# The second forward twiddle of two convolutions, read in 32 transfers of 1024-byte rows or in 4 of 8192-byte rows

## The chip, the cores and the metric

One core of one Trainium2 chip runs the whole program. The metric is the device time of one execution in microseconds. The engines work in parallel, each in the order of its own instructions: TensorE multiplies matrices (PE in the profile, its weight loads PEld), VectorE (DVE) and ScalarE (ACT) work element by element, GpSimd (POOL) does some set-up, and SyncE (SP) issues the transfers, which 16 DMA engines carry out.

## The reference

The input x has 2048 rows of 512 values. Four residual steps follow each other, two of each kind, with the same weights in both rounds:

```python
x = x + _A_ref(_layernorm(x), wqkv, wo)
x = x + _B_ref(_layernorm(x), A_re, A_im, B_re, B_im, C_re, C_im, log_dt, Dskip)
x = x + _A_ref(_layernorm(x), wqkv, wo)
x = x + _B_ref(_layernorm(x), A_re, A_im, B_re, B_im, C_re, C_im, log_dt, Dskip)
```

Step A is local attention: 32 heads of 16 channels, each position looks at 8 positions (itself and every second one before it). Step B is a long convolution along the 2048 positions, one filter for each of the 512 channels:

```python
P = jnp.exp(logdA[:, :, None] * l[None, None, :])
K = jnp.einsum("dn,dnl,dn->dl", Cc, P, dB).real
Kf, Uf = rfft(pad(K)), rfft(pad(u))
y = irfft(Uf * Kf)[:, :, :L] + u * Dskip
```

## The kernel before

**The stages.** The program first builds the filter K (function k_gen, 0 to about 107 us) together with the first parts of the first attention, then runs attention 1 (LayerA.core, to about 186 us), convolution 1 (FftB, to about 247 us), attention 2 (to about 351 us) and convolution 2 (to the end). The order of the instructions on each engine is written out by hand, as strings of one letter for each operation (CORE0 and CORE1 for the attentions, ORDER0, ORDERF and ORDER1 for the convolutions).

**The convolution.** The Fourier transform of 4096 points is done as two steps of matrix products. The first step (f1, L807) multiplies the data by a fixed 128 x 128 table and leaves 128 groups e for each of 64 sets of channels (a1s). The second step (f2, L814) multiplies each group e by a matrix of its own, 128 x 128: this is the second forward twiddle, a table w2 of 128 x 128 x 128 bf16 values, 4 MB. A call of f2 handles 16 groups (EC), with one weight load and one product for each group. Eight calls cover the 128 groups for one half of the channels. In convolution 1 both the filter (k_f2, letter k) and the data (u_f2, letter u) go through it, 32 calls; in convolution 2 only the data, 16 calls, since the spectrum of the filter is kept in DRAM. Then VectorE multiplies the spectra (u_mult, L852), and two inverse steps follow (i1 at L879 and L883, i2 at L908 to L929, with the table g2).

**The table w2.** It is written to DRAM in the first 50 us (L1425 fills it with zeros, L709 stores the sines) with the layout [128 partitions, 128 groups, 128], so that one partition's row is 32 KB. Each convolution reads it into SBUF anew, by load_w2 (L591 to L596): the tile w2_sb (w_sb in the profile) takes the place of the keys' tile of the attention (kT_ext, tag "slot"), so the read can start only when the last product of queries and keys (prod, L342) of that attention is done. The read is issued by the letter w in CORE0 and CORE1, in the middle of the attention's second half. The first 32 KB of a partition of this tile hold the table, and the rest (w2_rest) serves as one more buffer for filter spectra: in convolution 1 as the first of the buffers of spare(), in convolution 2 as one slot of the ring (ring_extra).

**What is around it on SP's queue.** SP issues in order. In attention 1 the loads of the filter's rows (k_load, L1362 and L1378) stand ahead of w2; behind it stand the load of the inverse table g2 (L766, first read by i2 at 232.5 us) and the copies that swap the halves of the filter's spectrum (kf_load, L839). In attention 2 seven slots of the ring (L842, L844) are loaded ahead of w2; behind it come the three slots w2_rest and kx (L842, L844, from 338.56 us), and then the slots that become free as u_mult goes on (from 362.9 us).

**Semaphores of the transfers.** In the compiled program the transfers of SP use eight semaphores in turn. Each transfer waits, ahead of its issue, until the transfer eight places earlier has landed. An instruction that reads transferred data waits for the semaphore of its transfer: weight loads of L814 wait for the transfer that holds their group e, which with 4 transfers is the first weight load of groups 0, 32, 64 and 96.

Of the kernel before, what the change touches and what calls it, by code (L numbers as in the profile page):

```python
# [199 lines left out]
class LayerA:  # L200
# [390 lines left out]
    def load_w2(self, w2_dram):  # L591
        w2 = self.keep.tile([P, NDT * (2 * D + (NA + 14) * P)], BF16, name="w2_sb", tag="slot")
        self.w2 = w2[:, 0:P * P].rearrange("p (e c) -> p e c", c=P)
        self.w2_rest = w2[:, P * P:]
        for c in range(4):
            self.nc.sync.dma_start(self.w2[:, c * 32:(c + 1) * 32, :], w2_dram[:, c * 32:(c + 1) * 32, :])  # L596

    def spare(self):

# [985 lines left out]
```

## Time and profile before

| | |
|---|---|
| runs before, median of 3 | 404.5 us (403.28 to 405.28) |
| profiled execution, whole | 400.43 us |
| its span, first to last instruction | 398.7 us |
| granted TensorE clock | 0.997 |
| w2 issued in attention 1, first read | 166.75 us, 192.45 us |
| w2 issued in attention 2, first read | 324.16 us, 359.11 us |
| w2, 1 MB transfer, issue to landing | 7.6 us (median) |
| bytes moved in the span | 54.16 MB |

The profile's times count from the first instruction of the span. Lines of a timeline give start and duration in us, then engine, line, operation, out<-in and the number of instructions merged in the line. SPq is SP's queue: the duration is that of the issuing instruction, and the transfer itself runs on after it. A table by stretches gives for each engine the busy time and, in brackets, the number of instructions (PE, PEld, DVE, ACT, POOL), then the granted clock, the busy share of the DMA engines and their GB/s. Idle time in square brackets comes with what ended it.

### The profile page before, as it was taken

Reading aid. Unit: us, or ns where it says so; the run is one execution under the profiler, and the core shown is the slowest. Engines: PE = TensorE matmul, PEld = TensorE weight load, DVE = VectorE, ACT = ScalarE, POOL = GpSimd, SP = SyncE. Lnnn points to the kernel's source line nnn. Section 1 sums busy time; section 2 is a strip of 40 time slices with the busy share of each in tenths; the row PEclk is TensorE's granted clock in tenths of the full one; section 3 lists DMA queues with packets and bytes.
Section 4 is the critical chain, followed back from the end, with each engine's and each line's share of the span. In section 5 each row is a group of like instructions: output and inputs, shape, how many; then the busy total and the mean of one; then the engine's idle time right before and its main releaser. Section 6 shows DMA issues by size and latency. Waiting matters only on the chain.

```text
span 398.7 us, 14678 instructions
## 1 busy us (share of the span) xinstructions
PE 324.2 (81%) x6456; PEld 231.7 (58%) x6503; DVE 373.8 (94%) x450; ACT 327.7 (82%) x561; POOL 62.9 (16%) x75
## 2 busy tenths in 40 slices
PE   3000079899999999989998798999999999998895
PEld 2000037557634766666887798553456767667795
DVE  6999999999999999998999889978999999989985
ACT  7999999997556679979999896764656878899993
POOL 9302930000399000300500000100000001000000
PEclk9999999999999999999999999999999999999998
DMA  7942820313015756493236684650063037503716
GB/s 222 392 138 37 92 67 11 85 41 95 14 41 132 199 174 193 111 399 113 76 126 245 247 275 108 237 161 2 2 170 95 3 123 305 161 3 97 224 34 183
DMA packets 62322, 54.16 MB, mean 136 GB/s; under 512 B 33869, under 2 KB 50738, under 8 KB 60978
## 3 DMA queue, kind: packets, MB, share of 16 engines
q1 hardware_dynamic: 62250, 53.22, 43.9%
q8 instruction: 50, 0.82, 0.9%
q14 instruction: 14, 0.11, 0.1%
q10 hardware_dynamic: 8, 0.00, 0.0%
HBM read 30.15 MB, written 13.24 MB: 109 GB/s over the span
## 4 chain that ended last, share of the span: by engine, by line
PE 49%; DVE 28%; issue 10%; ACT 8%; DMA 2%; SPq 2%; POOL 1%; DVEq 0%; ACTq 0%; POOLq 0%
PE pq L398 7%; PE pk L1273 5%; PE pq L508 5%; DVE pav L472 4%; PE po L497 4%; PE pq L223 4%; DVE prod L342 3%; DVE B_t L1115 3%; PE pp L282 3%; DVE A_t L1115 3%; PE pp L1211 3%; DVE a1s L796 3%; DVE t L852 2%; PE pb L807 2%; ACT ub L865 2%
## 5 line engine op out<-in xcount | busy, mean ns | idle before, releaser
L472 DVE TENSOR_TENSOR pav<-attn,v_ext 128x4096 bf16<-128x4096 bf16 (+1 forms) x34 | 72.1, 2156 | 0.0
L342 DVE TENSOR_TENSOR prod<-qT,kT_ext 128x4096 bf16<-128x4096 bf16 x29 | 66.1, 2311 | 3.5 <-PE L L350 1.4
L1201 PE MATMUL pt<-ident,x_blk 128*128 128x128 bf16 x64 | 5.8, 241 | 42.2 <-ACT x_blk L195 42.2
L1115 DVE TENSOR_TENSOR A_t<-A_t,pow_t 128x1024 bf16<-128x1024 bf16 (+4 forms) x46 | 37.7, 869 | 0.2
L508 PE MATMUL pq<-wop,oT 128*128 128x512 bf16 x121 | 31.3, 379 | 2.5 <-issue 2.1
L400 ACT CAST v_ext<-pq 128x512 bf16<-128x512 f32 x32 | 18.6, 585 | 16.6 <-PE pq L398 13.4
L865 ACT CAST ub<-pb 128x1024 bf16<-128x1024 f32 x32 | 31.8, 1081 | 0.3
L497 PEld LDWEIGHTS <-pav 64*128 64x128 bf16 x1664 | 25.9, 95 | 9.4 <-issue 6.1
L398 PE MATMUL pq<-wv,xnT 128*128 128x512 bf16 x120 | 30.4, 379 | 0.8 <-ACT kgs L1281 0.3
L814 PE MATMUL pb<-a1s,w_sb 128*128 128x64 bf16 x768 | 27.1, 193 | 3.8 <-ACT a1s L796 1.7
L1201 PEld LDWEIGHTS <-x_blk 128*128 128x128 bf16 x64 | 4.6, 108 | 43.9 <-ACT x_blk L195 43.2
L796 ACT CAST a1s<-pb 128x1024 bf16<-128x1024 f32 x30 | 29.0, 1066 | 0.9 <-PE pb L807 0.8
L497 PE MATMUL po<-ident,pav 64*128 64x64 bf16 x1664 | 28.8, 190 | 0.2 <-ACT oT L499 0.2
L1211 PE MATMUL pp<-xnT,kT_ext 128*128 128x512 bf16 x88 | 24.4, 393 | 4.9 <-ACT kT_ext L1216 2.4
L814 PEld LDWEIGHTS <-w_sb 128*128 128x128 bf16 x768 | 24.8, 98 | 5.8 <-issue 4.2
L1273 PEld LDWEIGHTS <-A_t 128*64 128x64 bf16 (+1 forms) x512 | 21.7, 103 | 4.3 <-DVE A_t L1115 0.5
L1273 PE MATMUL pk<-B_t,A_t 128*64 128x84 bf16 (+1 forms) x512 | 23.5, 201 | 0.4 <-DVE A_t L1115 0.4
L223 PE MATMUL pq<-xnT,kT_ext 128*128 128x512 bf16 x89 | 23.0, 379 | 0.5 <-issue 0.2
L178 POOL TENSOR_TENSOR ln_rstd<-ln_rstd,ln_mh 128x4 f32<-128x4 f32 x2 | 4.0, 2014 | 119.6 <-DVE ln_msq L170 83.6
L796 DVE CAST a1s<-pb 128x1024 bf16<-128x1024 f32 x18 | 21.2, 1214 | 1.8 <-PE pb L807 1.7
L398 PEld LDWEIGHTS <-xnT 128*128 128x128 bf16 x128 | 11.7, 97 | 14.3 <-issue 1.9
L508 PEld LDWEIGHTS <-oT 128*128 128x128 bf16 x128 | 12.5, 98 | 12.4
(257 smaller groups left out, 919.8 us busy)
## 6 DMA issues: line engine op xcount, KB each, us to landing
w_sb<-w_dram SPq DMA_DIRECT2D x8, 1024.0 KB, 7.6
w_dram<-xnT SPq DMA_DIRECT2D x1, 4096.0 KB
kf_ring<-kf_dram SPq DMA_DIRECT2D x13, 256.0 KB, 3.6
kf_ring<-kf_dram SPq DMA_DIRECT2D x26, 128.0 KB, 3.6
v_ext<-v_ext SPq DMA_DIRECT2D x4, 784.0 KB, 6.2
x_blk<-in_A_x_dram SPq DMA_DIRECT2D x4, 512.0 KB, 4.1
kT_ext<-in_A_wqkv_dram SPq DMA_DIRECT2D x4, 512.0 KB, 9.6
x_sb<-in_A_x_dram SPq DMA_DIRECT2D x4, 512.0 KB, 5.8
```

The costliest lines, as they stand in the source:

```text
L223: nc.tensor.matmul(pq[:], lhsT=self.wqk[:, dt, ft * P:(ft + 1) * P], rhs=self.xnT[:, dt, q * 512:(q + 1) * 512], start=(dt == 0), stop=(dt ...
L342: nc.vector.tensor_tensor(pr, self.qT[q][:, ft].unsqueeze(1).to_broadcast([P, W, 4, P]), kap, ALU.mult)
L398: nc.tensor.matmul(pp[:], lhsT=xnT[:, dt, a * P:(a + 1) * P], rhs=wv[:, dt, :], start=(dt == 0), stop=(dt == NDT - 1))
L472: nc.vector.tensor_tensor(pv[:, i], attn[:, n % 4].unsqueeze(2).to_broadcast([P, W, DH // parts, H]), vap, ALU.mult)
L497: nc.tensor.matmul(po[:, h, 0, i * nt + ft, :], lhsT=pvf[rows, i, w, ft * P:(ft + 1) * P], rhs=ident[rows, rows], start=(w == 0 and ft + i ...
L508: nc.tensor.matmul(pw[:], lhsT=oT[:, ftp, :], rhs=self.wo[:, ftp, :], start=False, stop=(ftp == NDT - 1))
L796: (self.nc.scalar.copy if eng == "act" else self.nc.vector.tensor_copy)(dst, src)
L814: nc.tensor.matmul(p2[:, j, :], lhsT=self.w2[:, ec * EC + j, :], rhs=a1s[:, ec * EC + j, :], start=True, stop=True)
L865: nc.scalar.copy(ub[:], p2)
L1115: return lambda: nc.vector.tensor_tensor(*args)
L1211: nc.tensor.matmul(pps[kind, b, ft][:], lhsT=la.wqk[:, dt, c:c + P], rhs=la.xnT[:, dt, b * 512:(b + 1) * 512], start=(dt == 0), stop=(dt = ...
L1273: nc.tensor.matmul(o, lhsT=lhs, rhs=Bt[:, ri, c * CH + ql].rearrange("p b g -> p (b g)"), start=(not half and j % 4 == 0 and ri == 0), sto ...
```

## The change

Each partition's 32 KB of w2 are read in 32 pieces of four groups (1024 bytes) in place of 4 pieces of 32 groups (8192 bytes). Each piece is one transfer over all 128 partitions. This holds for both convolutions, as both call load_w2.

```diff
@@ -592,8 +592,8 @@
         w2 = self.keep.tile([P, NDT * (2 * D + (NA + 14) * P)], BF16, name="w2_sb", tag="slot")
         self.w2 = w2[:, 0:P * P].rearrange("p (e c) -> p e c", c=P)
         self.w2_rest = w2[:, P * P:]
-        for c in range(4):
-            self.nc.sync.dma_start(self.w2[:, c * 32:(c + 1) * 32, :], w2_dram[:, c * 32:(c + 1) * 32, :])
+        for c in range(32):
+            self.nc.sync.dma_start(self.w2[:, c * 4:(c + 1) * 4, :], w2_dram[:, c * 4:(c + 1) * 4, :])
 
     def spare(self):
```

In the compiled order the 32 transfers stand on SP's queue where the 4 stood. The instructions of the other engines are the same and in the same order. What differs on them is what they wait for: 56 more weight loads of L814 wait for a transfer, since each piece now has its own.

## Prediction

> **What bounds the kernel now.** I read the page first: busy shares, then the chain that ended last.
>
> ```profile
> span 398.7 us, 14678 instructions
> PE 324.2 (81%) x6456; PEld 231.7 (58%) x6503; DVE 373.8 (94%) x450; ACT 327.7 (82%) x561; POOL 62.9 (16%) x75
> PE 49%; DVE 28%; issue 10%; ACT 8%; DMA 2%; SPq 2%; POOL 1%; DVEq 0%; ACTq 0%; POOLq 0%
> ```
>
> VectorE is busy 94% of the span, and the chain is TensorE and VectorE for 77%. Transfers and the SP queue hold 2% each, in the first convolution (206 to 221 us), where it copies and stores its spectrum. The changed transfers aren't on the chain. So the question is how much time lies between them and their first reader, and what stands behind them on SP. That is read in the timeline of SP, once for each convolution:
>
> ```profile
> 166.75 2.02 SPq L596 DMA_DIRECT2D w_sb<-w_dram  x4
> 183.98 0.32 SPq L766 DMA_DIRECT2D g_sb<-g_dram  x1
> 194.17 1.36 SPq L839 DMA_DIRECT2D w_sb<-w_sb  x2
> ...
> 324.16 2.68 SPq L596 DMA_DIRECT2D w_sb<-w_dram  x4
> 338.56 0.52 SPq L842 DMA_DIRECT2D w_sb<-kf_dram  x1
> 339.12 1.24 SPq L844 DMA_DIRECT2D w_sb<-kf_dram  x2
> ```
>
> and in that of TensorE's weight loads, which read the table (w_sb):
>
> ```profile
> 192.45 0.52 PEld L814 LDWEIGHTS <-w_sb 128*128 128x128 bf16 x16
> 194.10 1.09 PEld L814 LDWEIGHTS <-w_sb 128*128 128x128 bf16 x32
> 201.33 3.62 PEld L814 LDWEIGHTS <-w_sb 128*128 128x128 bf16 x112
> ...
> 359.11 0.52 PEld L814 LDWEIGHTS <-w_sb 128*128 128x128 bf16 x16
> 361.39 1.46 PEld L814 LDWEIGHTS <-w_sb 128*128 128x128 bf16 x48
> ```
>
> First issue to first reader: 192.45 - 166.75 = 25.7 us, and 359.11 - 324.16 = 35.0 us. On SP the first load is followed by one transfer (g_sb, first read at 232.5) and then by nothing until 194.17; the second by the ring loads at 338.56, which wait for the table to land because one ring slot lies in its tile.
>
> **The change, step by step.** Per convolution 4 transfers of 1 MB become 32 of 128 KB. Bytes and destination stay; no compute instruction is added, removed or reordered on any engine.
>
> *Issue.* The rows that bound one 128 KB issue (the source views of L596 and of L308; the three times are min, median, max in ns):
>
> ```profile
> L596 SPq DMA_DIRECT2D w_sb<-w_dram x8: 349/460/1271, 166.8 to 326.4; - x8
> L308 SPq DMA_DIRECT2D wop<-in_A_wo_dram x8: 597/641/2285, 125.1 to 241.5; - x8
> DMA to landing us min/median/max: 4.0/4.3/5.7
> ```
>
> L596 issues 128 rows each, as the new ones do: 2.02 / 4 = 0.505 us each in the first load, with the gaps. L308 moves what a new transfer moves, 128 KB in 1024-byte rows: 4 in 2.62 us = 0.655 each. I take 0.505, since the partition and row counts are those of L596, and keep 0.655. 32 x 0.505 = 16.2 us (21.0) in place of 2.0 and 2.7.
>
> *Moving.* Rows of 1024 bytes go nearly as fast as those of 8192. The stretch 170 to 175 us holds almost only the table's rows, 241 to 242 almost only 1024-byte weight rows (the last two numbers are DMA share and GB/s):
>
> ```profile
> 170.00:175.00 5.00, 4.68 (x186) 3.34 (x180) 5.00 (x3) 4.34 (x13) 0.00 (x0) 1.00 1.01 416
> 241.00:242.00 1.00, 1.00 (x21) 1.00 (x19) 1.00 (x3) 0.90 (x2) 0.00 (x0) 1.00 1.07 370
> ```
>
> At 370 GB/s, 131 KB take 0.35 us, less than one issue, so SP's issue sets the pace: the load is spread over 16 to 21 us at 200 to 260 GB/s where it took 10 to 13 us.
>
> *Eight at a time.* In the compiled order the transfers take eight semaphores in turn, and each waits until the one eight before it has landed. Eight issues are 8 x 0.505 = 4.0 us (5.2), against 4.3 us to landing in L308's row. So this wait adds little: at worst a landing of 5.7 us sets the pace, 5.7 / 8 = 0.71 us, 22.8 us in all.
>
> *First convolution.* Last issue at 166.75 + 16.2 = 182.9 (189.6 at worst), landed 4.3 us later, at 187.2 (193.9). The first reader wants only the first four transfers at 192.45; the last four are wanted by the last 16 loads of the x112 row, at 204.4. The g_sb load, now at 183.98, moves by 0 to 6 us and has 48 us to its reader. L839 at 194.17 finds SP free at either pace. Cost 0.
>
> *Second convolution.* Last issue at 340.4 (347.0), landed at 344.7 (351.3), against 359.11. The ring loads behind it (nine transfers, 338.56 to 344.84) move by about 6 us (13): issued until 351.0 (357.6), landed by 355.6 (362.2). VectorE first reads one of them at 370.74 (t from w_sb). Slack 8 to 15 us. Cost 0.
>
> *TensorE's waits.* In the compiled order 28 more weight loads per convolution wait on a transfer's semaphore, every fourth load in place of every 32nd. Two such waits stand inside the rows above: the 17th load of the x32 and the 33rd of the x48 (1.09 / 32 = 34 ns and 1.46 / 48 = 30 ns a load, as in the x112 row's 32 ns). So a wait that is met long before costs nothing to see. Upper bound: SP's own semaphore instructions at L596 take 17 to 28 ns; 56 x 0.028 = 1.6 us. I take 0, since the rows show the very instruction, and keep 1.6.
>
> *Less crowding.* VectorE doesn't feel the transfers: in its timeline five pav products from 164.52 take 11.09 us, under the table's load, and three from 142.91 take 6.68: 2.22 and 2.23 us each. If TensorE's small "issue" gaps under the two loads (groups by line, 166 to 186 us: 1.7 us ahead of L497's weight loads and 0.8 ahead of L508; 324 to 340 us: 0.4 and 0.3) came from it, 3.2 us could go; on the chain only 0.7 us of such gaps stand between 176 and 185 us. I take 0.
>
> Sum: 0, between -3.2 and +1.6 us.
>
> The Trainium skill, "DMA: Bandwidth & Descriptors", speaks against the change twice. Under "Bandwidth" it says to batch transfers to at least 1 MiB, and "Anatomy of one DMA" gives about 2.0 us fixed for each besides the bytes at 436 GB/s. By that, 32 one after another would be an estimated 32 x 2.3 = 74 us; the trace has four L308 issues in 2.62 us, so fixed parts overlap here. "Latency and other measured facts" lists large power-of-two row pitches that slow loads to 207 down to 103 GB/s, the smallest listed being 512 KiB; the table's rows lie 32 KiB apart before and after, and at that pitch the trace has 416 GB/s, though with 8192 bytes of each row.
>
> **The rivals.**
>
> *A slow pace (slower).* Place: SP's queue during the two loads. If a 1024-byte-row transfer at this pitch costs 1.25 us (L596's own longest issue is 1.271, L308's 2.285), the load takes 40 us. The point from which it decides: the last transfer must land by 204.4, so the pace must be under (204.4 - 4.3 - 166.75) / 32 = 1.04 us; L839 begins to start late from (194.17 - 0.3 - 166.75) / 32 = 0.85. Price at 1.25: first convolution 166.75 + 40 + 4.3 = 211.1, late by 6.7; second: table landed at 368.5, first ring load issued after it (1.8) and landed (4.3) at 374.6, against 370.74, late by 3.9. Together +10.6: 415 us on the scale of the runs shown. For it: the two long issues, and that eight in flight make the pace hang on landing times. Against: the medians 460 and 641 are far under 1.04, and 370 GB/s leaves no backlog.
>
> *The waits on TensorE (slightly slower).* At 28 ns or some more each, partly on the chain: +1.6 to +3, 406 to 407.5 us. For it: TensorE holds 49% of the chain. Against: the x32 and x48 rows.
>
> *Less crowding (faster).* -0.7 to -3.2: 401.3 to 403.8 us. For it: the gaps lie in the loaded stretch. Against: such gaps stand elsewhere too, and engine times don't change under load.
>
> *The change doesn't do what it says.* The compiled order has the 32 transfers in the place of the 4, so no.
>
> **How the numbers follow.** The profiled execution took 400.43 us (span 398.7, 1.7 around it); the runs shown have a median of 404.5, 4.1 more. By the profile's own time I forecast 400.4 + 0; on the scale of the runs, 404.5 us. A measurement of this kernel can tell 0.5%, 2 us, from no change. No change, with the runs' own spread (403.28 to 405.28), is 402.5 to 406.5: chance 0.58, of which 0.03 falls out on either side of 0.5%. Slow pace 0.14, all over. Waits on TensorE 0.14, of which 0.08 over. Less crowding 0.14, of which 0.07 by more than 2 us. That gives slower 0.03 + 0.14 + 0.08 = 0.25, faster 0.03 + 0.07 = 0.10, same 0.65. The range takes in no change, the waits and most of the crowding, and of the slow pace only a pace just above 1.04 us: 402 to 409.
>
> **What would show it.** SP: 32 L596 issues in 16 to 21 us at 0.5 to 0.65 each, ending before 189 and 346 us; the DMA rate in those stretches about half of 416; L766 no later than 190; L839 still near 194; the ring loads from about 345; weight loads still 30 to 34 ns apart in rows of 32 and more, and no new idle time at L814. I am wrong if the L596 pace is over 0.85 us, if TensorE's idle time at L814 grows, or if an operation that I hold untouched changes its duration.

## The result, and the profile after

| | before | after |
|---|---|---|
| median of 20 runs each | 403.98 us (401.31 to 408.01) | 401.64 us (399.28 to 404.87) |
| ratio, with its interval | | 0.995 [0.9927, 0.9973] |
| profiled execution, whole | 400.43 us | 400.23 us |
| its span | 398.7 us | 398.5 us |
| stage 1: pav at 164.52 to a1s at 191.82 in before | 27.30 us | 26.21 us |
| w2 issued in attention 1, first read | 166.75, 192.45 us | 168.76, 192.95 us |
| w2 issued in attention 2, first read | 324.16, 359.11 us | 324.44, 359.40 us |

The change makes the kernel faster by 2.3 us, half a per cent. The forecast was no change. Medians here and below are of all runs, while the ratios leave out the few runs that were over 1.5% above the fastest of their kernel. The two profiled executions are nearly equal (0.2 us apart) and hide the gain, since that of before was faster than any of the 20 runs in the table (400.43 against a median of 403.98). "Stage 1" is used throughout: the time on VectorE from the pav product that starts at 164.52 us in before to the cast into a1s that starts at 191.82, so the second half of attention 1, in which w2 is loaded, up to the first step of the convolution.

First the page of after, the same lines as were shown of before, and the group of VectorE's pav products:

```profile
span 398.5 us, 14735 instructions
PE 324.4 (81%) x6456; PEld 231.7 (58%) x6503; DVE 373.7 (94%) x450; ACT 328.0 (82%) x561; POOL 62.9 (16%) x75
PE 47%; DVE 25%; ACT 10%; SPq 7%; issue 7%; DMA 3%; POOL 1%; DVEq 0%; ACTq 0%; POOLq 0%
L472 DVE TENSOR_TENSOR pav<-attn,v_ext 128x4096 bf16<-128x4096 bf16 (+1 forms) x34 | 72.1, 2156 | 1.5 <-DMA v_ext<-v_ext 1.5
```

Busy times are the same within 0.3 us: on no engine did the work itself become shorter or longer. The last line tells why this execution isn't shorter than that of before: VectorE waited 1.5 us for a copy of v_ext, at 130.8 us, long before the changed load. Its stage from 107 to 131 us took 26.25 us, against 24.6 to 25.2 in all other runs, one of which (r1_both) builds the same loads. So this is a chance of one execution, and its 1.6 us outweigh the 1.1 us that stage 1 gave.

The chain asks for care. SPq has 7% now, 4% of it at L596, as if the issues were on the path. At 185.92 us VectorE's copy into k_perm (L1455) waits for the transfers of its input k_rl, on all eight semaphores. They were met long before, and the profile puts the wait down to the latest landing on such a semaphore, which is one of w2. VectorE had no idle time ahead of that copy (its timeline has no bracket there), so the chain steps through L596 without anything having waited for it.

Next SP's timeline of after, and the source view of L596:

```profile
168.76 19.56 SPq L596 DMA_DIRECT2D w_sb<-w_dram  x32
188.43 0.36 SPq L766 DMA_DIRECT2D g_sb<-g_dram  x1
194.66 1.18 SPq L839 DMA_DIRECT2D w_sb<-w_sb  x2
...
324.44 17.27 SPq L596 DMA_DIRECT2D w_sb<-w_dram  x32
344.84 0.52 SPq L842 DMA_DIRECT2D w_sb<-kf_dram  x1
```

```profile
L596 SPq DMA_DIRECT2D w_sb<-w_dram x64: 320/430/1738, 168.8 to 341.4; - x64
DMA to landing us min/median/max: 2.3/2.8/5.0
```

The pace is 19.56 / 32 = 0.61 us and 17.27 / 32 = 0.54 us, a transfer lands in 2.8 us, L839 starts 0.49 us later than before (with the stages ahead of it, which run later too), and the ring loads start at 344.84. And TensorE's weight loads of L814, in its timeline:

```profile
192.95 0.52 PEld L814 LDWEIGHTS <-w_sb 128*128 128x128 bf16 x16
194.60 1.09 PEld L814 LDWEIGHTS <-w_sb 128*128 128x128 bf16 x32
201.83 3.62 PEld L814 LDWEIGHTS <-w_sb 128*128 128x128 bf16 x112
```

The durations are those of before to the hundredth, with eight times as many waits in them. So in this profile the table is never late and the waits cost nothing. What was gained lies elsewhere, in stage 1. TensorE's timeline of before has there, ahead of the products that close a half of the heads (L487):

```profile
175.97 0.10 PEld L487 LDWEIGHTS <-pav 128*128 128x128 bf16 x1
177.60 1.77 PEld L487 LDWEIGHTS <-pav 128*128 128x128 bf16 x31 [1.53 <-issue]
```

and that of after in the same place:

```profile
177.84 1.99 PEld L487 LDWEIGHTS <-pav 128*128 128x128 bf16 x32
```

Before, TensorE stops for 1.53 us between the first and the second of 32 like weight loads, and the profile knows nothing that it waits for ("issue"). After, the 32 run through. In before's view of waits between 164 and 192 us the stop and what it holds up stand together (engine, line, what it waits for: us in total, times, longest):

```profile
ACT oT L489 <- PE po L487: 1.6, 1, 1.6
PEld L487 <- issue: 1.5, 1, 1.5
```

ScalarE waits for the products, VectorE a little later for ScalarE's sums (0.52 us ahead of L138) and for L807's product (0.46 us). Of the 1.09 us by which stage 1 is shorter, VectorE's two waits are 0.98.

### The profile page after: what moved, and what is told of

It is laid out like the page before. It is cut to its first block, busy times and chain, and to the rows that moved or that the text cites. A ratio compares the mean times of both kernels' runs of the same rounds, so it can differ in the third digit from the quotient of the medians.

```text
span 398.5 us, 14735 instructions
## 1 busy us (share of the span) xinstructions
PE 324.4 (81%) x6456; PEld 231.7 (58%) x6503; DVE 373.7 (94%) x450; ACT 328.0 (82%) x561; POOL 62.9 (16%) x75
## 4 chain that ended last, share of the span: by engine, by line
PE 47%; DVE 25%; ACT 10%; SPq 7%; issue 7%; DMA 3%; POOL 1%; DVEq 0%; ACTq 0%; POOLq 0%
PE pq L398 6%; PE pk L1273 5%; PE pq L508 4%; PE po L497 4%; SPq L596 4%; PE pq L223 3%; DVE B_t L1115 3%; DVE prod L342 3%; ACT ub L865 3%; PE pp L282 3%; DVE t L852 3%; DVE A_t L1115 3%; PE pp L1211 3%; SPq L1378 3%; DVE a1s L796 2%
## 5 line engine op out<-in xcount | busy, mean ns | idle before, releaser
L508 PE MATMUL pq<-wop,oT 128*128 128x512 bf16 x121 | 31.3, 379 | 2.5 <-issue 2.1
L400 ACT CAST v_ext<-pq 128x512 bf16<-128x512 f32 x32 | 18.6, 585 | 16.6 <-PE pq L398 13.4
L497 PEld LDWEIGHTS <-pav 64*128 64x128 bf16 x1664 | 26.0, 95 | 10.0 <-issue 5.7
L814 PE MATMUL pb<-a1s,w_sb 128*128 128x64 bf16 x768 | 27.1, 193 | 4.0 <-ACT a1s L796 1.7
L497 PE MATMUL po<-ident,pav 64*128 64x64 bf16 x1664 | 29.0, 190 | 0.6 <-DVE pav L472 0.4
L814 PEld LDWEIGHTS <-w_sb 128*128 128x128 bf16 x768 | 24.8, 98 | 6.0 <-issue 4.4
L1211 PE MATMUL pp<-xnT,kT_ext 128*128 128x512 bf16 x88 | 24.6, 397 | 4.5 <-ACT kT_ext L1216 2.0
L225 ACT CAST qT<-pq 128x512 bf16<-128x512 f32 x24 | 14.1, 585 | 6.9 <-PE pq L223 6.6
```

The costliest lines, as they stand in the source:

```text
L497: nc.tensor.matmul(po[:, h, 0, i * nt + ft, :], lhsT=pvf[rows, i, w, ft * P:(ft + 1) * P], rhs=ident[rows, rows], start=(w == 0 and ft + i ...
L508: nc.tensor.matmul(pw[:], lhsT=oT[:, ftp, :], rhs=self.wo[:, ftp, :], start=False, stop=(ftp == NDT - 1))
L814: nc.tensor.matmul(p2[:, j, :], lhsT=self.w2[:, ec * EC + j, :], rhs=a1s[:, ec * EC + j, :], start=True, stop=True)
L1211: nc.tensor.matmul(pps[kind, b, ft][:], lhsT=la.wqk[:, dt, c:c + P], rhs=la.xnT[:, dt, b * 512:(b + 1) * 512], start=(dt == 0), stop=(dt = ...
```

## The experiments

All ratios are to the kernel before, run on the same chip in the same set of runs.

### Is it real, and which of the two loads gives it?

All four kernels of this group write the number of transfers per convolution, and nothing else differs:

```diff
-        for c in range(4):
-            self.nc.sync.dma_start(self.w2[:, c * 32:(c + 1) * 32, :], w2_dram[:, c * 32:(c + 1) * 32, :])
+        n = (32, 4)[self.layer]
+        m = P // n
+        for c in range(n):
+            self.nc.sync.dma_start(self.w2[:, c * m:(c + 1) * m, :], w2_dram[:, c * m:(c + 1) * m, :])
```

with (4, 4) in r1_null, (32, 32) in r1_both, (32, 4) in r1_first and (4, 32) in r1_second.

> The kernel before, built again under another name: 4 transfers in both convolutions. It measures what two sets of runs of one program differ by. Theory A (the gain of 0.5% is real and belongs to the split load): ratio to before 1.000, within about 0.003. Theory B (the gain is a difference between two sets of runs): a ratio as far from 1 as 0.995 can show here too.

> The change itself, run again on one chip beside the kernel before. Theory A: ratio about 0.995 (2 us less). Theory B: 1.000 within the interval.

> 32 transfers in convolution 1 alone, 4 in convolution 2. Theory A1 (the load under attention 1 disturbs something that the split load leaves alone; there TensorE's last products lie on the path from 176 us on): 0.995. Theory A2 (it is the load under attention 2): 1.000. Theory B: 1.000.

> 32 transfers in convolution 2 alone, 4 in convolution 1. Theory A1: 1.000. Theory A2: 0.995. Theory B: 1.000.

| kernel | transfers, conv. 1 / 2 | median us | ratio | stage 1, us | stop ahead of L487, us |
|---|---|---|---|---|---|
| r1_null | 4 / 4 | 404.64 | 1.0008 [0.9974, 1.0042] | 29.32 | 2.1, and 1.2 in L497 |
| r1_both | 32 / 32 | 401.66 | 0.9944 [0.9909, 0.9979] | 26.21 | none |
| r1_first | 32 / 4 | 402.14 | 0.9932 [0.9899, 0.9965] | 26.31 | none |
| r1_second | 4 / 32 | 403.36 | 0.9993 [0.9964, 1.0022] | 28.70 | 2.1 |

The gain is real, and within the intervals all of it comes from convolution 1's load. Over the profiles of this group and the pair before and after, stage 1 takes 27.30, 29.32 and 28.70 us with 4 transfers there, 28.4 on average, and 26.2 to 26.3 with 32: 2.2 us less, about as much as the medians of the table differ (404.0 against 401.9 us on average). The stage with convolution 2's load (305 to 345 us) takes 39.8 us in all of these. Stage lengths are from one profile each, and the rest of a profile can hide the gain: between 205 and 239 us the profiles of r1_both, r1_first and r1_second are 4.1, 4.9 and 3.1 us longer than before's, those of after and r1_null are not, and these three were slower executions than the median of their kernel. In that stretch they have a stop of TensorE of 1.6 to 1.7 us and 4 us or more with the granted clock at 0.60 to 0.88. Whether the change makes such losses more or less frequent isn't shown; the medians hold whatever they cost.

r1_null shows more than before did. TensorE stops twice, in its timeline:

```profile
172.65 0.23 PEld L497 LDWEIGHTS <-pav 64*128 64x128 bf16 x11 [0.42 <-issue]
174.06 0.84 PEld L497 LDWEIGHTS <-pav 64*128 64x128 bf16 x53 [1.18 <-issue]
...
178.05 0.10 PEld L487 LDWEIGHTS <-pav 128*128 128x128 bf16 x1
180.25 1.77 PEld L487 LDWEIGHTS <-pav 128*128 128x128 bf16 x31 [2.10 <-issue]
```

(The 0.42 us that stand ahead of each group of L497 are always there, in after too; they are not the stops.) Counted from the program's start, the first stop follows weight load 1885 and the second weight load 2013, exactly 128 loads later, and neither is at the start of an operation of the program. What comes in such portions is the program itself. The page before has its transfers in a row of their own:

```profile
q8 instruction: 50, 0.82, 0.9%
```

50 transfers of 0.82 / 50 = 16.4 KB. TensorE has 6503 weight loads, 50.8 times 128, and a product for each. So q8 brings TensorE's instructions, one transfer for 128 weight loads and their products. The trace has when each transfer ran, and it bears this out: numbered in order, the transfers of before fit the places 128 loads apart on which 1885 and 2013 lie, each of the 50 ending 0.6 us or more before TensorE goes on past its place. Around the load of w2 (us):

```
kernel      instruction transfers       apart   TensorE's stop        its end after the transfer's end
before      168.88-170.26 175.25-176.35  6.37   175.97-177.60 (2013)  1.25
r1_null     162.70-163.76 171.25-172.68         172.78-174.06 (1885)  1.38
            171.25-172.68 177.69-178.72  6.44   178.06-180.26 (2013)  1.54
r1_second   170.42-171.75 176.72-177.74  6.30   177.14-179.34 (2013)  1.60
after       171.31-172.43 175.12-176.12  3.81   none (0.32 at 173.53) 1.42
r1_both     168.97-170.10 173.47-174.40  4.50   none
r1_first    170.03-171.85 174.84-175.92  4.81   none
```

A stop ends 1.25 to 1.6 us after an instruction transfer has ended. TensorE uses 128 weight loads in 4.0 to 4.7 us there (1885 at 171.96, 2013 at 175.97 in before). With the load in 4 transfers the next instructions come 6.3 to 6.4 us after the ones before, so it runs dry. With 32 they come after 3.8 to 4.8 us.

**First explanation:** instructions travel on the same 16 DMA engines as the data, and wait there. What they wait for is the question of the next group. The Trainium skill, "Runtime: NRT & Kernel Launch", section "Instruction fetch mechanics", says that instructions come in blocks of 16 KiB, 256 each, which the trace bears out (16.4 KB, 128 weight loads and 128 products). It also calls the cost of passing from one block to the next mostly hidden; under the load of w2 in 4 transfers it isn't, with stops of up to 2.1 us in this group.

### What makes the instructions late: long rows, long transfers or full engines?

All four kernels change convolution 1's load alone. The destination, the bytes and the place on SP's queue stay.

```diff
# r2_rows16k: 2 transfers of 2 MB, rows of 16384 bytes
+            m = P // 2
+            for c in range(2):
+                self.nc.sync.dma_start(self.w2[:, c * m:(c + 1) * m, :], w2_dram[:, c * m:(c + 1) * m, :])
# r2_strided: 4 transfers of 1 MB, each eight rows of 1024 bytes a partition
+            a, b = (v.rearrange("p (j c e) x -> p c j (e x)", c=4, e=4) for v in (self.w2, w2_dram))
+            for c in range(4):
+                self.nc.sync.dma_start(a[:, c], b[:, c])
# r2_part16: 32 transfers of 128 KB, each 16 partitions with rows of 8192 bytes
+            for c in range(4):
+                for g in range(0, P, 16):
+                    self.nc.sync.dma_start(self.w2[g:g + 16, c * 32:(c + 1) * 32, :], w2_dram[g:g + 16, c * 32:(c + 1) * 32, :])
# r2_n16: 16 transfers of 256 KB, rows of 2048 bytes
+            m = P // 16
+            for c in range(16):
+                self.nc.sync.dma_start(self.w2[:, c * m:(c + 1) * m, :], w2_dram[:, c * m:(c + 1) * m, :])
```

> In convolution 1 the table comes in 2 transfers with rows of 16384 bytes; convolution 2 as before. In the three profiles with 4 transfers TensorE stands still once at L487 (issue, 1.5 to 2.1 us, after the 358th weight load from 164 us on), about 1.3 to 1.6 us after an instruction transfer of 16 KB has ended that came 6.3 to 6.5 us after the one before it; in the three with 32 it doesn't, and the distance is 3.8 to 4.8 us. Theory H (the instruction transfer waits on its DMA engine behind the rows that one table transfer has put there, 8 rows of 8 KB = 64 KB, 2.5 us at 410 GB/s over 16 engines): 128 KB, 5 us, so the stall at L487 is 3 to 5 us and the time 0.5 to 1% over before. Theory R (it waits behind one row, 0.3 us at 8 KB): 0.3 us more, time within 0.2% of before. Theory L (it is the load on the DMA engines as such, 410 GB/s): stall and time as before.

> In convolution 1 the table comes in 4 transfers of 1 MB, but each of rows of 1024 bytes (128 partitions x 8 rows, 4096 bytes apart), 64 rows for each DMA engine; convolution 2 as before. Theory H: 64 KB stand in front as before, stall at L487 1.5 to 2.5 us, time as before (ratio 1.000). Theory R: rows are short, no stall, ratio 0.993 to 0.995. Theory L: rate stays at 350 to 410 GB/s, stall and time as before.

> In convolution 1 the table comes in 32 transfers of 128 KB with rows of 8192 bytes, 16 partitions each, one row for each DMA engine; convolution 2 as before. Theory H: 8 KB in front, no stall at L487, ratio 0.993 to 0.995. Theory R: rows as before, stall 1.5 to 2.1 us, ratio 1.000. Theory L: the issue sets the pace (about 250 GB/s), no stall, 0.993 to 0.995.

> In convolution 1 the table comes in 16 transfers of 256 KB with rows of 2048 bytes; convolution 2 as before. Issue at about 0.5 us each allows 520 GB/s, so the DMA engines stay full. Theory H: 16 KB in front, 0.6 us, no stall at L487, ratio 0.993 to 0.996. Theory R: the same. Theory L: engines as full as before, stall and time as before (1.000).

| kernel | row, bytes | transfers | median us | ratio | stage 1, us | stop at L487, us |
|---|---|---|---|---|---|---|
| r2_rows16k | 16384 | 2 of 2 MB | 402.71 | 0.997 [0.9943, 0.9998] | 30.63 | 2.4 |
| r2_strided | 1024 | 4 of 1 MB | 404.28 | 1.0012 [0.9981, 1.0043] | 29.76 | 2.4 |
| r2_part16 | 8192 | 32 of 128 KB | 405.58 | 1.0025 [0.9991, 1.0059] | 27.57 | 1.8 |
| r2_n16 | 2048 | 16 of 256 KB | 402.87 | 0.9973 [0.9947, 1.0] | 27.96 | 1.3 |

r2_strided has the rows of the change and stops as long as rows of 16 KB make it stop: the length of a row isn't it (theory R, though R alone had forecast the stop of r2_part16). r2_part16 has the number and the size of the change's transfers, and stops too: neither is it how much one transfer lays on an engine (theory H). What goes with the stop is in the stretches (the last two numbers are the busy share of the DMA engines and GB/s; the share can pass 1 a little). Before:

```profile
172.00:174.00 2.00, 1.84 (x68) 1.22 (x61) 2.00 (x2) 1.81 (x5) 0.00 (x0) 1.00 1.02 426
174.00:176.00 2.00, 1.84 (x69) 1.43 (x70) 1.97 (x5) 1.81 (x5) 0.00 (x0) 1.00 1.01 414
176.00:178.00 2.00, 0.75 (x10) 0.47 (x9) 1.86 (x3) 1.78 (x7) 0.00 (x0) 1.00 0.99 406
```

r2_part16:

```profile
172.00:174.00 2.00, 2.00 (x69) 1.25 (x63) 2.00 (x2) 1.85 (x5) 0.00 (x0) 1.00 1.13 172
174.00:176.00 2.00, 2.00 (x70) 1.40 (x70) 1.99 (x4) 1.78 (x5) 0.00 (x0) 1.00 0.96 139
176.00:178.00 2.00, 0.46 (x4) 0.18 (x3) 1.84 (x3) 1.82 (x7) 0.00 (x0) 1.00 0.86 143
```

After:

```profile
172.00:174.00 2.00, 1.72 (x45) 0.95 (x40) 2.00 (x2) 1.73 (x6) 0.00 (x0) 1.00 0.76 228
174.00:176.00 2.00, 1.84 (x64) 1.17 (x60) 2.00 (x2) 1.39 (x5) 0.00 (x0) 1.00 0.89 271
176.00:178.00 2.00, 1.84 (x68) 1.41 (x70) 1.82 (x6) 1.94 (x6) 0.00 (x0) 1.00 0.64 182
```

The third line of the first two is the stop: 10 and 4 products in 2 us, where after has 68. r2_part16 moves fewer bytes a second than after, 139 to 172 GB/s against 182 to 271, and stops all the same; its transfers keep the engines occupied (0.86 to 1.13). After leaves them free for a tenth to a third of the time (0.64 to 0.89) in these stretches, and the instructions get through; in the one before, 170 to 172 us, it has 1.05, and a gap of 0.22 us follows at 173.6. r2_n16 lies between in the length of its stop (1.3 us), with its engines full at 306 to 399 GB/s. So what goes with the stop is the occupancy of the engines, not bytes a second. Theory L had put it as bytes a second and so had forecast no stop for r2_part16: there it failed, and the reading by occupancy was made after these runs. For r2_n16 it had forecast the stop of before, and the stop was a little shorter.

How long the instructions wait can be read from the start of their transfer. As a rule it starts once TensorE has begun the block ahead of it: 0.6 to 0.9 us later with the engines nearly idle (in before, after weight loads 2141, 2269 and 2397, share 0.09 to 0.13). From the moment at which TensorE goes on past weight load 1885 to the start of the transfer for the loads after 2013, the wait was 2.9 to 3.9 us, at a share of 1.01 to 1.09, in the seven kernels that stop at L487, and 1.2 to 1.6 us, at 0.70 to 0.98, in the six that don't. The transfer itself then took 0.9 to 1.5 us. It isn't a sharp line: with 32 transfers the wait was up to 3.1 us at other places of the load (r1_both at 187.59 us, share 0.90), and a stop of 0.66 us followed there. So the change shortens the wait where it cost most, and doesn't end long ones. The Trainium skill, "DMA: Bandwidth & Descriptors", section "Queues, rings and completion order", says that an engine goes round its queues packet by packet. These runs don't show in what order an engine takes its packets; they show only that where the engines weren't quite full the block of instructions at L487 came some 2 us sooner.

r2_part16 is slow elsewhere as well. Its 32 issues take 25.91 us, 0.81 each, so its load reaches into the convolution, and in the stage after stage 1 (16.6 us, 13.0 in before) TensorE's timeline has

```profile
201.66 0.34 PEld L819 LDWEIGHTS <-w_sb 128*128 128x128 bf16 x7
204.30 4.58 PEld L819 LDWEIGHTS <-w_sb 128*128 128x128 bf16 x105 [2.30 <-issue]
```

L819 is L814 of before. This is not the table being late: the stop falls after the seventh load of a call of f2, and the 16 groups of a call lie in one quarter of the table, which those seven had already read. It is the same thing a third time: instruction transfers at 194.61 and then only at 201.90, done at 202.88, and the stop ends 1.42 us later. The engines' share between 198 and 202 us was 0.99 to 1.02, against 0.22 to 0.51 in before. The granted clock then fell to 0.53 and 0.61 (204 to 208 us), which adds to the 3.6 us.

Two points stay open here. r2_rows16k has the longest stage 1 in its profile and yet a ratio a little below 1, its interval ending just under it (0.9998); its one profile (404.92 us) is slower than its median. And in r2_rows16k and r2_strided the granted clock falls behind the stop, to 0.50 to 0.62, which goes with the rest of their long stages. r2_strided:

```profile
176.00:178.00 2.00, 0.33 (x2) 0.05 (x1) 1.86 (x3) 1.76 (x7) 0.00 (x0) 1.00 0.99 283
178.00:180.00 2.00, 1.57 (x25) 1.57 (x25) 1.89 (x4) 0.00 (x0) 0.00 (x0) 0.90 1.09 362
180.00:182.00 2.00, 2.00 (x13) 1.21 (x11) 0.99 (x1) 0.99 (x2) 0.00 (x0) 0.50 1.01 324
```

### Is it the portion of instructions, and does the rest of the gain add up?

r3_shift keeps before's 4 transfers and moves the portions: the first eight transposes are done five times over, 32 more weight loads and products at the start of the program, which write the same values again.

```diff
-            for di in range(2):
-                for a in range(4):
-                    nc.tensor.transpose(pt[:, di, a, :], xb[b][:, a, (2 * d + di) * P:(2 * d + di + 1) * P], ident[:])
+            for _ in range(5 if (b, d) == (0, 0) else 1):
+                for di in range(2):
+                    for a in range(4):
+                        nc.tensor.transpose(pt[:, di, a, :], xb[b][:, a, (2 * d + di) * P:(2 * d + di + 1) * P], ident[:])
```

r3_first is r1_first again, and r3_paced is r3_first with the weights of attention 2, which are loaded during convolution 1, in 8 transfers of 128 KB in place of 2 of 512 KB (r1_first has a stop of 1.6 us there, ahead of L885, L883 of before):

```diff
-        self.nc.sync.dma_start(self.wqk[:, :, D:2 * D], self.wsrc[:, :, D:2 * D])
-        self.nc.sync.dma_start(self.wqk[:, :, 0:D], self.wsrc[:, :, 0:D])
+        for c in (slice(D, 2 * D), slice(0, D)):
+            for dt in (slice(0, NDT),) if self.layer == 0 else (slice(i, i + 1) for i in range(NDT)):
+                self.nc.sync.dma_start(self.wqk[:, dt, c], self.wsrc[:, dt, c])
```

> The kernel before (4 transfers in both convolutions), with 32 more weight loads and 32 more products on TensorE: the first eight transposes of the filter stage's input (L1201, 51.8 us) are done five times over, where TensorE waits most of the time. So every later TensorE instruction stands 64 places further on in its stream. Theory F (the stall is a late instruction transfer of 16 KB, 256 instructions of 64 bytes, 128 weight loads and 128 products): the stall stays at the same place of the stream and so falls 32 weight loads earlier in the program: from L487 into the last quarter of the L497 group ahead of it, 1 to 2 us long, and none at L487's second weight load. Theory D (the stall belongs to what L487 reads or waits for): it stays at L487's second weight load. Time by both: before plus 0 to 2 us.

> 32 transfers in convolution 1 alone, once more, as the partner of the next kernel on the same chip: ratio to before 0.993 to 0.996; stage from 164.5 us (fifth last group of pav products) to 191.8 us (fourth a1s cast) 26.2 to 26.3 us, against 27.3 to 29.3 with 4 transfers.

> 32 transfers in convolution 1, and besides the weights of attention 2 (L254 and L255, 2 transfers of 512 KB with rows of 1024 bytes, issued at 233 us) in 8 transfers of 128 KB with the same rows, about 0.5 us apart. In the profiles of r1_first, r1_second and r1_both TensorE stood still for 1.7 to 1.8 us at L883 (238.7 to 240.3 us) while these two transfers were under way, and the stage from 224.3 to 239.0 us took 16.5 to 17.3 us; in before, after and r1_null it didn't, and it took 14.7. Theory L (a late instruction transfer where the DMA engines are full): no such stall here, the stage 14.7 us, the time 0 to 1 us under r3_first. If it is the rows' size and not the fullness: as r3_first.

| kernel | median us | ratio | stage 1, us | stop in stage 1 | stage 224 to 239, us |
|---|---|---|---|---|---|
| r3_shift | 406.87 | 1.0047 [1.0012, 1.0081] | 26.21 | none | 14.73 |
| r3_first | 401.48 | 0.9941 [0.9907, 0.9976] | 26.58 | none at L487, 0.6 in L497 | 16.43 |
| r3_paced | 401.36 | 0.9941 [0.9906, 0.9976] | 26.30 | none | 15.76 |

**r3_shift** was meant to move the stop into L497. It took it away. As a whole it is slower: the added work costs 4.2 us up to 107 us. But stage 1 takes 26.21 us, as long as with the change, although w2 is loaded in 4 transfers and the engines are full (0.88 to 1.04 between 176 and 182 us). Its timeline at the old place:

```profile
180.15 1.99 PEld L487 LDWEIGHTS <-pav 128*128 128x128 bf16 x32
```

The instructions for the loads after number 2013 came from 175.68 to 176.72, and TensorE got there at 178.75, 2.0 us after, so nothing was missing. The next came 6.25 us later, from 181.93 to 182.95, late as in before, and were wanted at 184.16: a gap of 0.24 us, its end 1.45 us after the transfer's. In before those 128 loads were wanted at 175.97, during the transfer. A stop of the same kind turned up elsewhere, after weight load 3677, where no other kernel has one:

```profile
244.96 0.10 PEld L928 LDWEIGHTS <-g_sb 128*128 128x128 bf16 x1 [1.39 <-issue]
```

The stretch from 239 to 247 us takes 9.38 us for it, against 7.95 in before. So the portions bear on where TensorE stops; where the stop falls was forecast wrongly, because I moved only the place in the program and not the time at which the block is fetched and the time at which it is used up. One thing isn't kept apart: in r3_shift w2 also starts later against the attention (173.8 us, 5.1 after the pav product that opens stage 1, in place of 2.2). The block that came late in before was fetched here early in the load: TensorE went on past weight load 1885 at 174.47, 0.7 us after the load's first issue, and the transfer started 1.2 us later. So this run shows that the stop depends on when fetch and load meet; how much of that is the moved portion isn't shown.

**r3_first** repeats the gain. Its stage 1 is 26.58 us where 26.2 to 26.3 was forecast: it has a stop of 0.63 us after weight load 1885, so with 32 transfers a short one can remain.

**r3_paced** has no stop ahead of that line in its profile; r3_first has, in their timelines:

```profile
236.20 1.42 PEld L885 LDWEIGHTS <-t 64*128 64x128 bf16 x93
239.30 1.04 PEld L885 LDWEIGHTS <-t 64*128 64x128 bf16 x67 [1.68 <-issue]
```

```profile
236.15 2.39 PEld L886 LDWEIGHTS <-t 64*128 64x128 bf16 x160
```

That is the mechanism at a second load (weight load 3549, again a multiple of 128 from the others). The forecast of 14.7 us for the stage was missed, with 15.76. And the two kernels can't be told apart, 401.36 and 401.48 us: before itself has no such stop in its profile, and r3_paced met a granted clock of 0.50 and 0.77 between 224 and 228 us. Whether such stops at this place cost anything on average isn't shown.

## Why the prediction was wrong, step by step

- *Issue*: right. 0.505 us each was forecast, 0.655 kept; 0.61 and 0.54 were measured, 19.6 and 17.3 us in place of 16.2 to 21.0.
- *Moving*: right on average. 4.19 MB in 19.56 us are 214 GB/s, and 182 to 271 in the stretches of 2 us; 200 to 260 was worked out. That step had the cause in its hand and drew nothing from it: at that rate the engines were no longer full (0.64 to 0.89).
- *Eight at a time*: right; a landing takes 2.8 us, less than L308's 4.3, and the pace stays under 0.71.
- *First convolution* and *Second convolution*, cost 0: right. No reader of w2 waited; the ring loads started at 344.84, 6.3 us later, where 6 were forecast.
- *TensorE's waits*, cost 0: right. The rows of 16, 32 and 112 weight loads have the durations of before.
- ***Less crowding*, "I take 0": this is the step that failed.** It was worth 2.2 us of stage 1 and the whole result. Three things were wrong in it. First, its evidence was that VectorE's products last as long under load as elsewhere. They do (11.09 us for five, after too), but what crowding delays is the supply of TensorE's instructions, and no operation's duration shows that. Secondly, it counted the wrong gaps: the 1.7 us ahead of L497 and 0.8 ahead of L508 are regular, and after has 2.3 and 0.8. The one that went, 1.5 us ahead of L487, wasn't in the sum, though it stood in the same view of groups by line:

```profile
L487 PEld LDWEIGHTS <-pav 128*128 128x128 bf16 x32 | 1.9, 98 | 1.6 <-issue 1.5
```

  Thirdly, it took the chain's 0.7 us as a measure of what could be won. Here are the chain's pieces of before at the stop (start, us, what):

```profile
176.62 0.58 ACT x_sb L514 x2
177.21 0.39 issue
177.60 1.95 PE po L487 x32
```

The 1.53 us appear as 0.39: the chain reaches the products by way of ScalarE's sums, which the first product waited for, and what of the stop lies beside those doesn't show. And one profiled execution was taken for the usual one; before's had a stop of 1.5 us, the other kernels with 4 transfers 2.1 to 2.4.

Of the rivals, *Less crowding* came true: 401.3 to 403.8 us, with a chance of 0.14. Its bounds hold the result, but they were made of the wrong gaps, so that is partly luck. *A slow pace* needed 1.04 us; the slowest run, r2_part16, had 0.81, and its cost came from its instructions, not from the table. *The waits on TensorE* are refuted by the rows. The range of 402 to 409 missed the 401.64 us because it left out the crowding's largest gains, 401.3 to 402 us.

One reading beside the sum was off and changed nothing in it. The Trainium skill, "DMA: Bandwidth & Descriptors", gives the fixed 2.0 us of its section "Anatomy of one DMA" for transfers that GpSimd issues, and the row pitches of "Latency and other measured facts" for copies from DRAM to DRAM; w2 is issued by SyncE and goes to SBUF. In this trace the quickest of the new transfers landed 2.3 us after its issue.

## What to carry to other kernels

A bulk load with time to spare need not be fast: spread it so that the DMA engines don't stand at a share of 1.0 while TensorE runs many short instructions, since those arrive over the same engines. Look for it as a single "issue" gap of 1 to 2.5 us in the middle of a run of like weight loads, compare the gap's end with the instruction transfers, and check it over several profiles, as each execution draws its own stops. By these runs it pays where TensorE uses up a block faster than a crowded fetch brings the next, 4.0 to 4.7 us against 5.3 to 6.9 here; convolution 2's load, where the same 128 loads take 6.5 to 7.5 us (number 4957 at 327.56, 5085 at 335.04 and 5213 at 341.52 in before), gave nothing.

## What the runs showed of the hardware that was not expected

- TensorE's instructions come 128 weight loads and their products at a time, in 16.4 KB, and barely ahead of their use: a transfer starts as a rule after TensorE has begun the block ahead of it, and a stopped TensorE goes on 1.2 to 1.6 us after the transfer has ended.
- With full DMA engines such a transfer started 2.9 to 3.9 us after the block ahead was begun, with rows of 1024 to 16384 bytes and transfers of 128 KB to 2 MB alike, in place of 0.6 to 0.9 with idle ones. The distance between two transfers under the load was 5.3 to 6.9 us in the kernels that stop at L487, 3.8 to 4.8 in those with 32 transfers over 128 partitions.
- Transfers over 16 partitions with rows of 8192 bytes occupy the engines (0.86 to 1.13) at only 139 to 202 GB/s, and are issued at 0.81 us each; transfers over 128 partitions with rows of 1024 bytes at 0.54 to 0.61.
- After a stop of 2.3 to 2.4 us the granted clock fell to between 0.50 and 0.62 for 2 us or more in three kernels (r2_strided, r2_rows16k, and r2_part16 at L819); after the shorter ones at L487 it stayed at 1.00. In r3_paced it fell to 0.50 at 224 us behind several gaps of 0.3 to 0.6 us, so the length of one stop alone doesn't set it; what does is open.
